# Three small changes of order in one kernel of attention and two expert layers: the held expert's products, the comparisons of the routing, and two places of weights

## The chip, the cores and the metric

The kernel runs on one core of a Trainium2 chip. The metric is the device time of one execution in microseconds (us), as the median of a few runs. The core's engines have queues of their own: TensorE (PE in the profile, with its weight loads as PEld), VectorE (DVE), ScalarE (ACT), GpSimd (POOL) and SyncE (SP), which here issues most transfers.

## What is computed

Three layers follow each other on 1152 tokens of 512 features.

```
x   = attention(q, k, v, s)                  # 2 x 8 heads, 576 positions, causal, a bias from s
e   = argmax(x @ w_gate)                     # first expert layer: one of 8 experts for each token
x1  = gate * (relu(x @ w1[e]) @ w2[e])       # at most 288 tokens for one expert
l   = x1 @ w_gate2                           # second layer: logits over 8 experts
# all (token, expert) pairs in falling order of l: a token takes the expert if it has
# none yet and the expert has fewer than 144 tokens
out = relu(x1 @ w1b[e2]) @ w2b[e2]           # 144 tokens for each of 8 experts
```

Each expert has a w1 of 512 x 1024 and a w2 of 1024 x 512 in f32, 2 MB each, 32 matrices in all.

## The kernel before

**Order.** The schedule is written out by hand: each engine runs its instructions in the order in which the program states them, and waits by semaphores where data or a buffer is missing. So a line that stands earlier in the program is earlier in the queue of its engine, and whatever stands behind a waiting instruction waits with it.

**Stages.** Attention runs until about 140 us. Then `for e in range(E)` runs the first layer's eight experts (146 to 270 us): `layer1` forms relu(x w1) in four steps of two column blocks, `second1` multiplies by w2. Then comes the routing's first phase (270 to 292 us), and from 298 us the second layer, `moe2`, in which the routing's later phases (`phases`, one `yield` at a time) run between the experts' products.

**Weights.** `load_part` fetches a matrix in four parts of 512 KB on SP's queue. `place(i)` says which 2 MB buffer matrix i goes to (i = 2e is w1 of expert e, i = 2e + 1 its w2): `ring[0]` and `ring[1]` exist from the start, `ring[2]`, `ring[3]`, `kept[0]` and `kept[1]` are laid where attention's tiles were, after `at.close()`. `load_next` issues parts in the order of `loads` as long as `free(i)` allows the next one and the expert's number is known; `quota` limits their number. One matrix that may not go stops all behind it. Before, w1 of the third expert (i = 4) goes to `ring[1]`, which holds w2 of the first, and so waits until `second1` of the first expert is over (`0 in given`). The f32 parts are split into a high half (ACT, line 160) and a low half (DVE, line 164) by `split_next`, at places of the experts' steps given in STEPS. The ACT's queue so holds splits, which wait for a transfer, ahead of the `h` and `y` copies that PE waits for.

**The held expert.** The last expert's second product (`held_steps`) is kept back and cut into 24 steps: 4 steps of 6 matmuls for each of 4 column blocks, with an ACT and a DVE step (`y`) behind each pair of blocks (20 steps), then `rows_steps`, 4 steps: 8 transposes on PE, then an ACT copy into `xo` and a scatter of rows to `x2d` in DRAM (`back1_out`, POOL line 1101), for each half of the tokens. FILL says after which step of the routing how many of them ("f") are issued; "r" are the same row steps of the expert before it.

**The routing's first phase.** For each of nine tiles of 128 tokens `compare(t)` writes a 128 x 1152 table of f16 (DVE line 1580; ACT line 1578 for tiles 1, 4 and 7) into one of five buffers `g`, and `products(g, t)` multiplies it on PE (line 1586, nine matmuls). The tiles come in the order 0 1 2 4 3 7 5 6 8. Comparisons were issued four tiles ahead of the products, in each round ahead of the products of that round. The maximum over the counts, the choice of the first full expert (`evi`), its weights (`known(0)`, two parts), and its token numbers (`tok`) follow. `gather` (POOL line 1443) reads the chosen rows from `x2d`, and so waits for all scatters into it. Behind the two gathers POOL writes a word `gone`, for which SP waits in `passed(9)` before it issues the next nine parts of weights. `warm(n)` issues n matmuls of 512 columns with no use but to occupy PE; WARM2 has their numbers at three places, the last ahead of `spread`, which turns the gathered rows for the second layer's first expert.

Of the kernel before, what the change touches and what calls it, by code (L numbers as in the profile page):

```python
# [9 lines left out]
F32 = mybir.dt.float32  # L10
F16 = mybir.dt.float16
BF16 = mybir.dt.bfloat16
# [9 lines left out]
def tile_attention_moe_moe(ctx: ExitStack, tc: tile.TileContext, q, k, v, s, wg1, w1a, w2a, capacity,  # L22
                           wg2, w1b, w2b, out, dbg=None):
    nc = tc.nc
    B, H, S, D = q.shape
    NTOK, DM = out.shape
    E = wg1.shape[1]
# [47 lines left out]
    ring = [ring_pool.tile([P, 4096], F32, name=f"wf{i}") for i in range(2)]  # L75
# [3 lines left out]
    WSP = [tuple(wsp0.tile([P, 4096], t, name=f"{n}{i}") for n, t in (("wh", F16), ("wl", BF16))) for i in range(2)]  # L79
    WS = {}  # L80

    FILL = ". rf rrrf ffff ffffff ffff ffff . . ff ff . . . . ."

# [7 lines left out]

    ONE = (E - 2, E - 1)

    WARM2 = (6, 5, 4)


    order = {}
# [5 lines left out]
    quota = [99]  # L105


    given = set()

    def place(i):  # L110

        e, k = divmod(i, 2)
        if k:
            return (ring[2:] + kept[:1])[(e - 1) % 3] if e else ring[1]
        return ring[(e + 1) % 2 if 0 < e < E else e % 2]

    def load_part(i, c):
        w, k = halves[i]
        t = loaded[i] = place(i)
        e = order[i // 2]  # L120
        src = (w[e:e + 1] if isinstance(e, int) else w[bass.ds(e, 1)]).rearrange("o (c p) f -> p (o c) f", p=P)
        n, f = src.shape[1:]
        t = t.rearrange("p (c f) -> p c f", c=n)
        if i // 2 == E:
            sl = (slice(None), slice(None), slice(c * f // 4, (c + 1) * f // 4))
        else:
            sl = (slice(None), slice(c * n // 4, (c + 1) * n // 4))
        nc.sync.dma_start(t[sl], src[sl])

    def free(i):  # L130

        e, k = divmod(i, 2)
        busy = lambda j: any(x[0] == j for x in split_queue + late)
        if k:
            return e == 0 or len(ring) > 2 and (e < 4 or e - 3 in given)
        return e == 0 or (0 in given if e == 2 else not busy(i - 2 if e == 1 else i - 4))

    def load_next():

        while quota[0] and loads:  # L140
            i = loads[0][0]
            if not (i < 2 or free(i)):
                break
            if i // 2 not in order and not (i < 2 * E and asked and asked[0](i // 2)):
                break
            load_part(*loads.pop(0))
            quota[0] -= 1

    def split_parts(i, part):
        x = loaded[i], *WS[i]  # L150
        if i % 2:
            return [a[:, part * 1024:(part + 1) * 1024] for a in x]
        return [a.rearrange("p (c f) -> p c f", c=4)[:, :, part * 256:(part + 1) * 256] for a in x]

    def split_hi(i, part):
        if part == 0:
            e, k = divmod(i, 2)
            WS[i] = (WSH if e in HELD else W2S[e % 2]) if k else WSP[e % 2]
        src, hi, lo = split_parts(i, part)
# [713 lines left out]
    if "XR" in dbg:  # L873
# [11 lines left out]
    kept = [wsp.tile([P, 4096], F32, name=f"wf{i}") for i in range(4, 6)]  # L885

    W2S = [tuple(kept[1].bitcast(t)[:, 4096 * i + j:4096 * i + j + 2048] for t, j in ((F16, 0), (BF16, 2048)))
           for i in range(2)]
    WSH = ring[1].bitcast(F16)[:, :4096], ring[1].bitcast(BF16)[:, 4096:]

    def open_pools(st, p, tag, names):
        for n, b in names:
# [106 lines left out]
    SL = C0 // 2  # L999
# [43 lines left out]
    mo1, mo2 = {}, {}  # L1043
# [42 lines left out]
    def back1_pe(ys, q_, x2f, l3):  # L1086
        w = x2f.shape[0]
        sl = slice(q_ * w, (q_ + 1) * w)
        for cp in range(2):
            pb = pbs.tile([P, 512], F32)[:w, :2 * (P + 2 * E)].rearrange("p (c d) -> p c d", c=2)  # L1090
            for c in range(2):
                nc.tensor.matmul(pb[:, c], ys[0][:, 2 * cp + c, sl], IW[:, 2 * cp + c], start=True, stop=False)
                nc.tensor.matmul(pb[:, c, :P + E], ys[1][:, 2 * cp + c, sl], IW[:, 2 * cp + c, :P + E],
                                 start=False, stop=True)
            nc.scalar.activation(x2f.rearrange("p (c d) -> p c d", c=4)[:, 2 * cp:2 * cp + 2], pb[:, :, :P],
                                 AF.Copy)
            nc.vector.reduce_sum(l3[:, cp], pb[:, :, P:].rearrange("p c (k e) -> p e c k", k=2), axis=AX.XY)  # L1097

    def back1_out(t, g, xo):
        nc.gpsimd.tensor_scalar(xo[:, DM + E:], g, 1.0 / XSC, None, op0=OP.mult)  # L1100
        i = nc.gpsimd.indirect_dma_start(  # L1101
            out=x2d[:, :], out_offset=bass.IndirectOffsetOnAxis(ap=t, axis=0),
            in_=xo, in_offset=None, bounds_check=NTOK - 1, oob_is_err=False)
        for o in scat2:
            tc.declare_no_dep(i.ins, o.ins, reason="distinct rows")
        scat2.append(i)

    def back1(ys, q_, t, g):


        w = g.shape[0]
        x2f, xo, l3 = (mo1["o"].tile([SL, n], F32, name=a)[:w]
                       for a, n in (("x2f", DM + E + 1), ("xo", DM + E + 1), ("l3", 3 * E)))
        x2f = x2f[:, :DM]
        l3 = l3.rearrange("p (k e) -> p k e", k=3)
        xo16 = xo.bitcast(F16)
        back1_pe(ys, q_, x2f, l3)
        nc.vector.tensor_add(l3[:, 2], l3[:, 0], l3[:, 1])
        nc.vector.tensor_scalar(xo[:, DM:DM + E], l3[:, 2], g, 1.0 / SG, op0=OP.mult, op1=OP.mult)
        nc.vector.tensor_copy(xo16[:, :DM], x2f)  # L1120
        nc.vector.tensor_sub(xo16[:, DM:2 * DM], x2f, xo16[:, :DM])
        back1_out(t, g, xo)

    def slots(r, q_):
        w = CAPS[r] // 2
        return tix[:w, r, q_:q_ + 1], gs[:w, r, q_:q_ + 1]
# [130 lines left out]
            yield from rows_steps(e, ys)  # L1257

    def rows_steps(e, ys):
        for q_ in range(NQ):  # L1260
            t, g = slots(e, q_)
            w = g.shape[0]
            xo = mo1["o"].tile([SL, DM + E + 1], F32, name=("xo", "x2f")[q_])[:w]
            pb = pbs.tile([P, 512], F32).bitcast(F16)[:w]
            for k in range(2):
                for c in range(4):
                    nc.tensor.transpose(pb[:, (4 * k + c) * P:(4 * k + c + 1) * P], ys[k][:, c, q_ * w:(q_ + 1) * w], ident)
            yield
            nc.scalar.activation(xo.bitcast(F16)[:, :2 * DM], pb, AF.Copy)
            nc.gpsimd.memset(xo[:, DM:DM + E], 0.0)  # L1270
            back1_out(t, g, xo)
            yield

    fills = FILL.split()

    def fill():
        for c in fills.pop(0):
            next(todo[c], None)
# [123 lines left out]
    rf = ctx.enter_context(tc.tile_pool(name="routef", bufs=1))  # L1402
# [158 lines left out]
    def ranks(pc, m, Bo, Bh, n, act_t, apart=3):  # L1561


        order = [t for t in range(n) if t not in act_t]
        for k, t in enumerate(act_t):
            order.insert(min(apart * k + apart - 1, len(order)), t)

        def head(first):
            for t in act_t:
                nc.tensor.matmul(pc, ones, Bh[:, t, None, :].to_broadcast([P, n, E]), start=first,  # L1570
                                 stop=False, skip_group_check=True)
                nc.tensor.matmul(pc[:, t], negi, Bh[:, t], start=False, stop=False, skip_group_check=True)
                first = False

        def compare(t):
            g = gp.tile([P, NTT, P], F16, name="g")[:, :n]
            if t in act_t:
                nc.scalar.activation(g, rowb[:, :n], AF.Sign, bias=m[:, t:t + 1], scale=-1.0)
            else:
                nc.vector.tensor_scalar(g, rowb[:, :n], m[:, t:t + 1], None, op0=OP.is_lt)  # L1580
            return g

        def products(g, t):
            rhs = Bh if t in act_t else Bo
            for i in range(n):
                nc.tensor.matmul(pc[:, i], g[:, i], rhs[:, t], start=False,
                                 stop=t == order[-1] and i == n - 1, skip_group_check=True)
        return head, order, compare, products
# [47 lines left out]
    def warm(n):  # L1636

        o = Banks("C1").tile([P, 512], F32)
        for _ in range(n):
            nc.tensor.matmul(o, ident, iotat[:, :512], start=True, stop=True)  # L1640
# [7 lines left out]
    head, tiles, compare, products = ranks(pc, m, Bo, Bh0, NTT, (1, 4, 7), 2)  # L1648
# [1 line left out]
    nc.gpsimd.tensor_sub(sres[:, 0], L2T, S3[:, 0])  # L1650
    nc.gpsimd.tensor_copy(S3[:, 1], sres[:, 0])
    nc.gpsimd.tensor_sub(S3[:, 2], sres[:, 0], S3[:, 1])
    AHEAD = 4
    gs_ = [compare(t) for t in tiles[:AHEAD]]
    head(True)
    for k, t in enumerate(tiles):
        if k + AHEAD < NTT:
            gs_.append(compare(tiles[k + AHEAD]))
        products(gs_[k], t)
        fill()  # L1660
    mx = rw.tile([P, NTT], F32, name="mx0")
    nc.vector.reduce_max(mx, pc, axis=AX.X)
# [23 lines left out]
    fill()  # L1686
    warm(WARM2[0])
    slot_pe(O0, R0, NTT)
    warm(WARM2[1])
    fill()  # L1690
# [241 lines left out]
    pop_lo()  # L1932
    warm(WARM2[2])
    XT1[0] = spread(xg.pop(0))
# [64 lines left out]
```

## Time and profile before

| | |
|---|---|
| time, median of 3 runs | 458.85 us (458.82 to 460.01) |
| the profiled execution: its own time | 456.74 us |
| its span, first to last instruction | 454.7 us |
| PE busy | 400.4 us, 88% of the span |
| PEld, DVE, ACT, POOL busy | 371.6, 309.2, 249.1, 190.9 us |
| DMA | 103.02 MB, mean 227 GB/s |

The span is that of the one execution that was profiled, and all positions below are us from its start. The shares are means over stages with different limits, so a stage is read by its own rows. Line numbers (L164) are those of the kernel before.

### The profile page before, as it was taken

The page shows a single profiled execution, that of the slowest core. Times are in us where ns is not written, and L with a number is a line of the kernel's source. Part 1 is how long each engine was busy: PE and PEld are TensorE (multiplying, and loading weights), DVE is VectorE, ACT ScalarE, POOL GpSimd, SP SyncE. Part 2 cuts the span into 40 slices and gives each one's busy share as a digit, 9 for nine tenths or more (in the row PEclk, how much of TensorE's full clock was granted, in tenths as well). Part 3 has the DMA queues.
Part 4 walks back from the last instruction along what each step waited for, and adds up shares of the span by engine and source line. Part 5 has one row for each costly group of instructions (what it writes and reads, how often), then busy time and mean ns, then how long its engine had stood idle before and what let it go on. Part 6 is the DMA issues. An engine that isn't in the chain of part 4 may idle for free. (4 is left out here: it accounts for less than half of the span.)

```text
span 454.7 us, 13676 instructions
## 1 busy us (share of the span) xinstructions
PE 400.4 (88%) x5260; PEld 371.6 (82%) x5260; DVE 309.2 (68%) x926; ACT 249.1 (55%) x459; POOL 190.9 (42%) x306
## 2 busy tenths in 40 slices
PE   1679999978989998999999999679989999999970
PEld 1457888867767998999999988379889999999960
DVE  7889999987776466876888956775855465465100
ACT  4447888855761546556667727153666466355420
POOL 4387888858822511402412624402432341441120
PEclk9979999989999999999999999969999999999995
DMA  7797999858915599999997930499996978987000
GB/s 156 170 206 175 194 223 223 208 157 274 329 32 224 157 343 400 346 349 353 385 318 167 155 63 27 129 274 319 371 391 176 334 246 262 311 294 246 30 25 20
DMA packets 94398, 103.02 MB, mean 227 GB/s; under 512 B 56136, under 2 KB 63304, under 8 KB 94323
## 3 DMA queue, kind: packets, MB, share of 16 engines
q1 hardware_dynamic: 88931, 91.85, 69.7%
q0 software_dynamic: 4192, 9.91, 7.1%
q8 instruction: 43, 0.70, 0.7%
q10 hardware_dynamic: 1200, 0.30, 0.3%
q14 instruction: 32, 0.26, 0.2%
HBM read 81.42 MB, written 14.59 MB: 211 GB/s over the span
## 5 line engine op out<-in xcount | busy, mean ns | idle before, releaser
L164 DVE TENSOR_TENSOR wl<-wf,wh 128x1024 bf16<-128x1024 f32 x64 | 77.7, 1234 | 25.0 <-ACT wh L160 23.9
L160 ACT ACTIVATE wh<-wf 128x1024 f16<-128x1024 f32 x64 | 65.7, 1051 | 23.5 <-DMA wf<-in_moe_w_dram 23.5
L988 PE MATMUL C<-h,wf 128*128 128x160 f32 (+7 forms) x544 | 58.6, 269 | 1.7 <-ACT h L942 1.7
L933 PE MATMUL A<-xt,wl 128*128 128x144 f16 (+4 forms) x288 | 59.5, 231 | 0.0
L931 PE MATMUL A<-xt,wh 128*128 128x144 f16 (+4 forms) x288 | 59.5, 231 | 0.0
L932 PE MATMUL A<-xt,wh 128*128 128x144 f16 (+4 forms) x288 | 59.5, 231 | 0.0
L1101 POOL DMA_INDIRECT x2d<-xo,tix x14 | 23.0, 1640 | 78.0 <-DVE l L1097 40.2
L932 PEld LDWEIGHTS <-wh 128*128 128x128 f16 x512 | 50.7, 99 | 1.1 <-issue 0.6
L933 PEld LDWEIGHTS <-wl 128*128 128x128 bf16 x512 | 50.8, 99 | 0.9 <-DVE wl L164 0.9
L931 PEld LDWEIGHTS <-wh 128*128 128x128 f16 x512 | 50.8, 99 | 0.2 <-issue 0.2
L536 ACT ACTIVATE pf<-pE,XB 128x512 f32<-128x512 f32 (+4 forms) x80 | 36.9, 515 | 9.7 <-PE pE L531 9.4
L1872 POOL DMA_INDIRECT out_dram<-x2f,tok x14 | 14.9, 1066 | 61.9 <-ACT h L942 34.3
L414 POOL TENSOR_TENSOR pl<-pf,ph 128x512 f16<-128x512 f32 x30 | 35.5, 1194 | 5.8 <-DVE ph L403 3.7
L988 PEld LDWEIGHTS C<-h,wf 128*128 128x128 f32 x256 | 36.2, 190 | 1.9 <-ACT h L942 1.9
L1852 PE MATMUL C<-h,wf 128*128 128x144 f32 x256 | 35.5, 290 | 2.0 <-ACT h L942 2.0
L488 DVE CUSTOM_DVE_ANT_0 junk<-pM,cb 128x128 f16<-128x128 f32 (+4 forms) x80 | 32.2, 431 | 6.5 <-PE pM L478 5.8
L1443 POOL DMA_INDIRECT xg<-x2d,tok x16 | 23.4, 1465 | 26.1 <-PE A L1145 8.9
L1852 PEld LDWEIGHTS C<-h,wf 128*128 128x128 f32 x256 | 32.5, 190 | 2.2 <-ACT h L942 2.2
L476 PE MATMUL pM<-al,ar 128*128 128x128 f16 (+2 forms) x96 | 27.5, 327 | 6.7 <-DVE rm L488 6.5
L559 PE MATMUL pog<-vf,pf 128*128 128x65 f32 x180 | 28.7, 282 | 0.0
L933 PE MATMUL C<-xt,wl 128*128 128x144 f16 x128 | 25.3, 230 | 0.7 <-DVE wl L164 0.7
L932 PE MATMUL C<-xt,wh 128*128 128x144 f16 x128 | 25.3, 230 | 0.0
(410 smaller groups left out, 1167.8 us busy)
## 6 DMA issues: line engine op xcount, KB each, us to landing
wf<-in_moe_w_dram SPq DMA_DIRECT2D x128, 512.0 KB, 10.0
xd<-zero SPq DMA_DIRECT2D x18, 257.0 KB, 4.5
cb<-cumd SPq DMA_DIRECT2D x16, 288.0 KB, 5.5
x2d<-zero SPq DMA_DIRECT2D x9, 260.5 KB, 3.4
kf<-in_k_dram SPq DMA_DIRECT2D x16, 128.0 KB, 4.4
vf<-in_v_dram SPq DMA_DIRECT2D x16, 128.0 KB, 4.3
qf<-in_q_dram SPq DMA_DIRECT2D x14, 128.0 KB, 3.2
bl<-al SPq DMA_DIRECT2D x16, 72.0 KB, 5.2
```

The source lines that it names most:

```text
L160: nc.scalar.activation(hi, src, AF.Copy)
L164: nc.vector.tensor_sub(lo, src, hi)
L414: (nc.gpsimd if ENG[name][i % 2] == "P" else nc.vector).tensor_sub(o, x, y)
L476: nc.tensor.matmul(o, AR[m][:, t * P:(t + 1) * P], AL[m][:, j0:j1], start=True, stop=not diag)
L488: nc.vector.tensor_tensor_reduce(junk[:w, :j1 - j0], o, CB[m][:w, j0:j1], 1.0, r if t == 4 and j0 == 0 else -3e38, OP.add, OP.max, r)
L536: nc.scalar.activation(d, o, AF.Exp, bias=x, scale=2.0 ** -13)
L559: nc.tensor.matmul(o, pf[:, c:c + P], VF[n % 4][:, j, h], start=False, stop=j == t)
L931: nc.tensor.matmul(ph[:, g], wh[:, c, fs], xt[:, c], start=c == 0, stop=False)
L932: nc.tensor.matmul(ph[:, g], wh[:, c, fs], xt[:, 4 + c], start=False, stop=False)
L933: nc.tensor.matmul(ph[:, g], wl[:, c, fs], xt[:, c], start=False, stop=c == 3)
L988: nc.tensor.matmul(py[:, g], a[:, f, d], b[:, f], start=k == 0, stop=k == len(terms) - 1)
L1852: nc.tensor.matmul(py[:, g], a[:, f, d], b[:, f], start=k == 0, stop=k == len(terms) - 1)
```

## The change

`place` exchanges two homes: the w1 matrices that went to `ring[1]` go to `kept[0]`, and the w2 matrices that went to `kept[0]` (fourth and seventh expert, and their like in the second layer) go to `ring[1]`, as does what follows from it in `free`: the third expert's w1 no longer waits for the first expert's w2, the fourth expert's w2 does. The held expert's split w2 (`WSH`) moves to `kept[0]`. Four parts of weights (w2 of the second expert) are issued as soon as the new buffers are declared, ahead of the loads of tokens. FILL puts 14 steps of the held expert, all that is left of its products, behind the products of the first tile, and its four row steps behind the fifth and sixth tile instead of the sixth and seventh. Comparisons go five tiles ahead, each issued behind a round's products. `rows_steps` issues POOL's memset and its scaling of the gates for both halves ahead of the transposes. The last of the three `warm` calls has 5 matmuls instead of 4.

```diff
--- before.py
+++ after.py
@@ -79,7 +79,7 @@
     WSP = [tuple(wsp0.tile([P, 4096], t, name=f"{n}{i}") for n, t in (("wh", F16), ("wl", BF16))) for i in range(2)]
     WS = {}
 
-    FILL = ". rf rrrf ffff ffffff ffff ffff . . ff ff . . . . ."
+    FILL = ". rf rrrf ffff ffffffffffffff . . . ff ff . . . . . ."
 
 
 
@@ -93,7 +93,7 @@
 
     ONE = (E - 2, E - 1)
 
-    WARM2 = (6, 5, 4)
+    WARM2 = (6, 5, 5)
 
 
     order = {}
@@ -111,8 +111,8 @@
 
         e, k = divmod(i, 2)
         if k:
-            return (ring[2:] + kept[:1])[(e - 1) % 3] if e else ring[1]
-        return ring[(e + 1) % 2 if 0 < e < E else e % 2]
+            return (ring[2:] + ring[1:2])[(e - 1) % 3] if e else ring[1]
+        return kept[0] if ((e + 1) % 2 if 0 < e < E else e % 2) else ring[0]
 
     def load_part(i, c):
         w, k = halves[i]
@@ -132,8 +132,8 @@
         e, k = divmod(i, 2)
         busy = lambda j: any(x[0] == j for x in split_queue + late)
         if k:
-            return e == 0 or len(ring) > 2 and (e < 4 or e - 3 in given)
-        return e == 0 or (0 in given if e == 2 else not busy(i - 2 if e == 1 else i - 4))
+            return e == 0 or len(ring) > 2 and (e < 3 or e - 3 in given)
+        return e == 0 or (len(ring) > 2 if e == 2 else not busy(i - 2 if e == 1 else i - 4))
 
     def load_next():
 
@@ -886,7 +886,11 @@
 
     W2S = [tuple(kept[1].bitcast(t)[:, 4096 * i + j:4096 * i + j + 2048] for t, j in ((F16, 0), (BF16, 2048)))
            for i in range(2)]
-    WSH = ring[1].bitcast(F16)[:, :4096], ring[1].bitcast(BF16)[:, 4096:]
+    WSH = kept[0].bitcast(F16)[:, :4096], kept[0].bitcast(BF16)[:, 4096:]
+
+    quota[0] = 4
+    load_next()
+    quota[0] = 99
 
     def open_pools(st, p, tag, names):
         for n, b in names:
@@ -1096,8 +1100,10 @@
                                  AF.Copy)
             nc.vector.reduce_sum(l3[:, cp], pb[:, :, P:].rearrange("p c (k e) -> p e c k", k=2), axis=AX.XY)
 
-    def back1_out(t, g, xo):
+    def back1_gate(g, xo):
         nc.gpsimd.tensor_scalar(xo[:, DM + E:], g, 1.0 / XSC, None, op0=OP.mult)
+
+    def back1_out(t, xo):
         i = nc.gpsimd.indirect_dma_start(
             out=x2d[:, :], out_offset=bass.IndirectOffsetOnAxis(ap=t, axis=0),
             in_=xo, in_offset=None, bounds_check=NTOK - 1, oob_is_err=False)
@@ -1119,7 +1125,8 @@
         nc.vector.tensor_scalar(xo[:, DM:DM + E], l3[:, 2], g, 1.0 / SG, op0=OP.mult, op1=OP.mult)
         nc.vector.tensor_copy(xo16[:, :DM], x2f)
         nc.vector.tensor_sub(xo16[:, DM:2 * DM], x2f, xo16[:, :DM])
-        back1_out(t, g, xo)
+        back1_gate(g, xo)
+        back1_out(t, xo)
 
     def slots(r, q_):
         w = CAPS[r] // 2
@@ -1257,18 +1264,22 @@
             yield from rows_steps(e, ys)
 
     def rows_steps(e, ys):
+        xs = []
         for q_ in range(NQ):
             t, g = slots(e, q_)
-            w = g.shape[0]
-            xo = mo1["o"].tile([SL, DM + E + 1], F32, name=("xo", "x2f")[q_])[:w]
+            xo = mo1["o"].tile([SL, DM + E + 1], F32, name=("xo", "x2f")[q_])[:g.shape[0]]
+            nc.gpsimd.memset(xo[:, DM:DM + E], 0.0)
+            back1_gate(g, xo)
+            xs.append((t, xo))
+        for q_, (t, xo) in enumerate(xs):
+            w = xo.shape[0]
             pb = pbs.tile([P, 512], F32).bitcast(F16)[:w]
             for k in range(2):
                 for c in range(4):
                     nc.tensor.transpose(pb[:, (4 * k + c) * P:(4 * k + c + 1) * P], ys[k][:, c, q_ * w:(q_ + 1) * w], ident)
             yield
             nc.scalar.activation(xo.bitcast(F16)[:, :2 * DM], pb, AF.Copy)
-            nc.gpsimd.memset(xo[:, DM:DM + E], 0.0)
-            back1_out(t, g, xo)
+            back1_out(t, xo)
             yield
 
     fills = FILL.split()
@@ -1650,13 +1661,13 @@
     nc.gpsimd.tensor_sub(sres[:, 0], L2T, S3[:, 0])
     nc.gpsimd.tensor_copy(S3[:, 1], sres[:, 0])
     nc.gpsimd.tensor_sub(S3[:, 2], sres[:, 0], S3[:, 1])
-    AHEAD = 4
+    AHEAD = 5
     gs_ = [compare(t) for t in tiles[:AHEAD]]
     head(True)
     for k, t in enumerate(tiles):
+        products(gs_[k], t)
         if k + AHEAD < NTT:
             gs_.append(compare(tiles[k + AHEAD]))
-        products(gs_[k], t)
         fill()
     mx = rw.tile([P, NTT], F32, name="mx0")
     nc.vector.reduce_max(mx, pc, axis=AX.X)
```

## Rows read from the trace of the kernel before

**Rows 1.** Windows of three stretches: busy us (instructions) by engine, PEclk, DMA share, GB/s

```profile
300.00:333.00 33.00, 29.58 (x410) 28.44 (x409) 23.80 (x99) 16.19 (x29) 8.78 (x12) 0.94 1.05 337
333.00:440.00 107.00, 105.78 (x1317) 104.51 (x1315) 52.59 (x170) 55.02 (x92) 32.06 (x33) 1.00 0.71 234
```

**Rows 2.** Waits of PE, 160 to 200 us: us in total, times, longest

```profile
PE C L988 <- ACT h L942: 1.7, 1, 1.7
PE D L1093 <- DVE y L991: 0.6, 1, 0.6
```

**Rows 3.** Timeline of ACT, 145 to 190 us: start, us, operation [idle before]

```profile
161.51 1.06 ACT L160 ACTIVATE wf<-wf 128x1024 f16<-128x1024 f32 x1 [1.65 <-DMA wf<-in_moe_w_dram]
...
171.80 1.06 ACT L160 ACTIVATE wh<-wf 128x1024 f16<-128x1024 f32 x1 [2.86 <-DMA wf<-in_moe_w_dram]
```

**Rows 4.** Timeline of SP's DMA queue, 100 to 260 us

```profile
134.67 1.97 SPq L128 DMA_DIRECT2D wf<-in_moe_w_dram  x4
151.96 1.37 SPq L1014 DMA_TRANSPOSE xt<-xd  x1
...
154.83 2.89 SPq L128 DMA_DIRECT2D wf<-in_moe_w_dram  x4
...
162.56 16.12 SPq L128 DMA_DIRECT2D wf<-in_moe_w_dram  x16
```

**Rows 5.** Timeline of PE, 160.5 to 174.5 us, up to the second expert

```profile
160.32 1.39 PE L988 MATMUL C<-h,wf 128*128 128x160 f32 x9
```

**Rows 6.** Line L1014 (transposed loads of tokens), issue to landing

```profile
DMA to landing us min/median/max: 7.1/9.2/11.1
```

**Rows 7.** Timeline of PE, 275 to 300 us

```profile
277.01 1.58 PE L1249 MATMUL C<-h,wf 128*128 128x136 f16 x24
278.43 0.37 PE L1586 MATMUL A<-Bh,g 128*128 128x8 f16 x9
...
280.31 0.87 PE L1249 MATMUL C<-h,wf 128*128 128x136 f16 x12
...
281.69 0.75 PE L1267 MATMUL D<-ident,y 128*68 128x128 f16 x8
```

**Rows 8.** Timeline of DVE, 240 to 302 us

```profile
275.90 2.28 DVE L1580 TENSOR_SCALAR g<-rowb,m 128x1152 f16<-128x1152 f32 x3 [1.38 <-ACT rowb L1148]
...
281.64 0.44 DVE L1255 SCALAR_TENSOR_TENSOR y<-C,y 128x272 f16<-128x272 f32 x1 [1.86 <-ACT y L1253]
282.00 1.54 DVE L1580 TENSOR_SCALAR g<-rowb,m 128x1152 f16<-128x1152 f32 x2
```

**Rows 9.** Timeline of POOL, 240 to 302 us

```profile
284.45 1.18 POOL L1101 DMA_INDIRECT x2d<-xo,tix  x1 [4.57 <-ACT x2f L1269]
...
286.28 1.55 POOL L1101 DMA_INDIRECT x2d<-x2f,tix  x1 [0.31 <-POOL x2f L1100]
292.81 1.06 POOL L1443 DMA_INDIRECT xg<-x2d,tok  x1 [4.98 <-DVE Bo L1739]
```

**Rows 10.** DMA issues, 284 to 294 us: median us to landing

```profile
x2d<-x2f,tix POOLq DMA_INDIRECT x1, 5.7
```

**Rows 11.** Half-microsecond windows around the fall of PE's clock

```profile
297.00:297.50 0.50, 0.07 (x2) 0.07 (x3) 0.09 (x1) 0.00 (x0) 0.00 (x0) 0.91 0.23 33
...
304.00:304.50 0.50, 0.50 (x9) 0.50 (x7) 0.50 (x5) 0.00 (x0) 0.00 (x0) 0.76 1.16 290
```

**Rows 12.** Timeline of PE, 275 to 300 us, behind the routing's first phase

```profile
293.06 1.03 PE L1640 MATMUL C<-iotat,ident 128*128 128x512 f16 x4
296.20 0.56 PE L1463 MATMUL A<-ident,xg 72*128 72x72 f16 x8 [2.12 <-ACT rowb L1148]
```

**Rows 13.** Timeline of SP's DMA queue, 296 to 300 us

```profile
296.15 5.66 SPq L128 DMA_DIRECT2D wf<-in_moe_w_dram  x5
```

**Rows 14.** Timeline of ACT, 300 to 345 us

```profile
331.13 1.06 ACT L160 ACTIVATE wh<-wf 128x1024 f16<-128x1024 f32 x1 [4.17 <-DMA wf<-in_moe_w_dram]
```

**Rows 15.** Timeline of PE, 332 to 338 us

```profile
332.54 0.76 PE L1852 MATMUL C<-h,wf 128*128 128x144 f32 x4 [1.97 <-ACT h L942]
```

## The prediction

> **What bounds the kernel now.** I read the page first: PE is busy for 88% of the span, and a kernel like that is bounded by PE wherever PE has no gap. So the next view is the list of PE's own gaps, stage by stage. Between 146 and 284 us they are few. In the first experts two stand out, 1.7 us and 0.6 us [rows 2]. The reader should see that both are named after an engine (ACT's `h`, DVE's `y`), though neither engine is short of time. ACT's timeline says what it did instead: at 171.80 a split of weights had waited 2.86 us for its transfer, at 161.51 another 1.65 us [rows 3], and the `h` and `y` copies stood behind them in ACT's queue. The queue of SP gives the origin: after the second expert's w1 at 134.67 nothing is issued until the loads of tokens at 151.96; w2 of the second expert goes at 154.83 and the third expert's w1 as late as 162.56 [rows 4].
>
> The second place is the routing's first phase. PE is nearly full until its last products, and then a chain of waits sets when the second layer begins. POOL's timeline shows its tail: the scatter of the held expert's second half starts at 286.28, and the first gather at 292.81 [rows 9]. The name behind that wait (a DVE operation) had long been done; the scatter takes 5.7 us to land [rows 10], which is 291.98, and from there to the gather's start are 0.8 us. Behind the two gathers SP is released and resumes the weights at 296.15 [rows 13].
>
> The third place is the beginning of the second layer. From 300 to 333 us the DMA share is 1.05 at 337 GB/s [rows 1]; at 331.13 ACT had waited 4.17 us for weights [rows 14], and PE 1.97 us for ACT [rows 15]. From 333 to 440 us PE is busy for 105.78 of 107 us [rows 1]. So what counts for the end is not when PE enters the second layer but when the weights of its third expert arrive, and these come from a stream that resumes at 296.15.
>
> **The change, part by part.**
>
> *Places of weights.* No operation is added or removed: the same 2 MB transfers go to other buffers. The third expert's w1 no longer waits for the first expert's w2 to be used, and the four parts of the second expert's w2 are issued where SP's queue was empty, from about 137 us (134.67 + 1.97, rows 4) instead of 154.83. The third expert's w1 then follows the loads of tokens at about 155 instead of 162.56. Seven us are more than both of ACT's waits (2.86 and 1.65 us, rows 3), so I take both PE gaps as gone: −1.7 − 0.6 = −2.3 us [rows 2]. What is late next? `ring[1]` now makes the fourth expert's w2 wait for the first expert, but that matrix stood behind the same wait before, as everything did. Loads of tokens now stand behind eight more parts on SP (for the third expert), which is not used until the second expert is over. The bounds are 0 (the parts do not come earlier) and −2.3 us; I take the latter, because the gaps have no second cause in the rows.
>
> *The held products.* Work is moved, not removed. Before, 60 matmuls ran in three batches from 277.01 with the products of two tiles between them; 24 take 1.42 us (277.01 to 278.43), a tile 0.23 us (278.43 to the next batch), and the last 12, which start at 280.31, end at 281.02 [rows 7]. In one piece they end at 277.01 + 60/24 × 1.42 = 280.56, 0.46 us earlier. DVE's `y` came 0.62 us behind their end (281.64) [rows 8], so now at 281.18.
>
> *The comparisons.* Being five ahead costs nothing by itself: `g` has five buffers, and the buffer is released by the same products as before. But DVE's queue now reads three comparisons, the two `y`, three comparisons. Before it was three, `y`, one, `y`, two. Behind the last `y` there are now three at 2.28 us instead of two at 1.54 us [rows 8]. The last comparison ends at 281.18 + 0.36 + 2.28 = 283.82 instead of 282.00 + 1.54 = 283.54: +0.3 us for the routing's maximum and for all that waits for it (counts, first full expert, its first two parts of weights). What hides these 0.3 us: the gather does not wait for the counts but for the scatter, and the stream behind it resumes by the gather. Without that cover they would be paid in full.
>
> *The rows and the scatter.* The transposes of the held rows began at 281.69 behind six tiles' products [rows 7]; now they stand behind five, at 280.56 + 4 × 0.23 = 281.48, with `y` complete some 0.4 us earlier. I take 0.3 us, so the first scatter starts at 284.15 instead of 284.45. The second starts today 0.65 us after the first ends (284.45 + 1.18 = 285.63 to 286.28, rows 9), because memset and scaling lie between; with both issued ahead only the wait of 0.31 us in its row is left, and it starts at 284.15 + 1.18 + 0.31 = 285.64, 0.64 us earlier. Landing after the same 5.7 us, it releases the gathers and then the stream 0.6 us earlier. Bounds: 0, if the landing is set by something else, and 1 us, if the scatter also lands faster away from the first weights. I take −0.6.
>
> One page would have it otherwise: the Trainium skill, "DMA: Bandwidth & Descriptors", section "Anatomy of one DMA — SWDGE (gpsimd) path", gives such a transfer about 2.0 us plus its bytes at 436 GB/s. For 68 rows of some 2 KB that is an estimate of 2.3 us, by which the scatter would have landed at 288.6, the gather would be waiting for something else, and the sum would lose its 0.6 us. The 5.7 us of rows 10 decide.
>
> *One more warm matmul.* Four of them took 1.03 us from 293.06; a fifth adds 0.26 us in a pause of PE that lasted until 296.20 [rows 12]. It costs nothing there. It might matter for the clock: that was at 2.4 GHz until 297.4 (0.91 granted in that half microsecond) and at 1.2 GHz until 304.2 (0.76 in that one) [rows 11], 6.8 us in which half the speed, 3.4 us of work, was lost. But PE reached its wait at 332.54 before its weights all the same, so by rows 14 and 15 an earlier PE would mostly wait longer. I take 0 of 3.4.
>
> **Sum.** −1.7 − 0.6 (first experts) − 0.6 (stream of the second layer) = −2.9 us. The profiled execution would go from 456.74 to 453.8 us. The median of the runs lies 2.1 us above it, which none of these rows explains; I take the difference off the median: 458.85 − 2.9 = 455.9 us.
>
> **Rivals.** A change of less than 0.3% (1.4 us) cannot be told from none here.
>
> *The clock stays up.* If PE's pause ahead of the second layer shrinks enough, the clock does not fall, the routing's next two phases, which name the second layer's next experts, come up to 3.4 us sooner, and with them part of the stream. For it: rows 11 and 12. Against it: the DMA queues are full from 300 to 333 us [rows 1]. About half of the 3.4 us would be kept: −2.9 − 1.6 = −4.5, 454.4 us. The Trainium skill, "TensorE: Matmul & The Clock Gate", Part 1, has activity release the throttle, which speaks for it; this trace agrees as far as the fall came behind a pause of PE.
>
> *Only one place pays.* The scatter's landing is not what holds the gather, or the first experts' 2.3 us are half lost to a new wait of ACT: −2.3 + 0.3 or about −2.0, 456.8 us.
>
> *The change does not do what it says.* If the new buffers lie on attention's tiles that are read until 152 us, the early parts are not early. Then only the 0.6 us and perhaps the small gap remain, less 0.3: 458.4 us.
>
> *Slower: tokens behind weights.* SP's queue is in order. If the four early parts still stand there at 151.96, the load of the second expert's tokens goes 2.89 us later [rows 4], behind 2.1 MB, which at 337 GB/s [rows 1] take 6.2 us, and lands 7.1 to 11.1 us after its issue [rows 6]. PE wants it at 160.32 + 1.39 = 161.7 [rows 5]. From 151.96 and 7.1 there are 2.6 us to spare; at worst PE stands 6.4 us. It decides from a stall of 4.3 us (2.9 gained, 1.4 more); taken with 4.5 to 5, the time is 460.5 us. Against it: the first of those buffers lies where attention's first tiles of queries, keys and values are, whose last use in the program is some heads before its end.
>
> **How the numbers follow.** Chances: forecast 0.50, clock stays up 0.14, one place only 0.12, not what it says 0.16, slower 0.08. The first three make it faster by over 0.3% (0.76), the fourth stays within (0.16), the last is slower (0.08). The predicted time is the likeliest case's, 455.9 us. The range reaches from below the rival with the clock (454.4, less 0.8 us for a scatter that lands faster and for the spread of the runs) to the case of no effect: 453.6 to 458.6 us.
>
> **What will show it.** ACT's splits at about 158 to 172 without a wait for weights, and PE's two gaps gone: the first step is right. SP's issue of four parts before 145 us: the places do what they say. DVE's three comparisons in one piece behind the second `y`, ending about 0.3 us later relative to the first held product, with the second scatter 0.6 us earlier: the routing is read rightly. A gather that starts less than 1 us behind the scatter's landing: the chain is right. And ACT still waiting for weights ahead of the third expert of the second layer, whatever the clock did: the clock is worth little. The prediction is wrong if PE shows a new gap ahead of the second expert, if the gather does not move, or if the wait for weights at 331 us moves by another amount than the gather.

## The result, and the profile after

| | median of the runs | profiled execution | its span |
|---|---|---|---|
| before | 458.84 us (458.46 to 460.01) | 456.74 us | 454.7 us |
| after | 453.12 us (451.90 to 454.15) | 452.32 us | 450.4 us |

The ratio is 0.9862, with a 95% interval of 0.9826 to 0.9898: 6.3 us faster (4.7 to 8.0), where 2.9 were forecast. The profiled executions differ by 4.4 us only. Ratios, here and below, leave out runs that lie over 1.5% above the fastest of the same kernel, and medians do not. The forecast of 455.9 us had the right side and too small a gain, and the time lies just below its range.

What the change says it does, it does, though the early parts go later than forecast. SP's queue after, to be held against [rows 4]; the second row, from a narrower window, shows the last four of the eight parts alone, and the row in the block below it is the wait of SP's queue ahead of them (us in total, times, longest):

```profile
134.79 11.10 SPq L128 DMA_DIRECT2D wf<-in_moe_w_dram  x8
143.79 2.11 SPq L128 DMA_DIRECT2D wf<-in_moe_w_dram  x4
156.76 1.29 SPq L1018 DMA_TRANSPOSE xt<-xd  x1
...
160.04 4.28 SPq L128 DMA_DIRECT2D wf<-in_moe_w_dram  x8
```

```profile
SPq L128 <- DVE ka L646: 6.5, 1, 6.5
```

Eight parts, not four, stand ahead of the loads of tokens. The first four are the second expert's w1, at 134.79 us as before. The second expert's w2 follows from 143.79 us, 11 us ahead of its place before (154.83): SP first waited 6.5 us for an operation of attention on DVE (`ka`, line 646). The third expert's w1 is issued from 160.04 instead of 162.56. ACT's timeline after shows what came of it at the two splits of [rows 3]:

```profile
158.70 1.99 ACT L160 ACTIVATE wf<-wf 128x1024 f16<-128x1024 f32 x2
...
168.94 1.05 ACT L160 ACTIVATE wh<-wf 128x1024 f16<-128x1024 f32 x1
```

There is no bracket behind the operations, so ACT did not wait ahead of them. The view of PE's waits, which showed the two gaps of [rows 2], is empty for 160 to 200 us. The loads of tokens go out later (156.76 instead of 151.96), and no gap of PE follows from that.

In the routing, PE's timeline after answers to [rows 7], with the held products in one piece:

```profile
275.54 3.71 PE L1256 MATMUL C<-h,wf 128*128 128x136 f16 x60
...
279.99 0.61 PE L1279 MATMUL D<-ident,y 128*68 128x128 f16 x8
```

DVE's timeline after answers to [rows 8]: three comparisons stand behind the last `y`, and the maximum behind them:

```profile
279.71 0.44 DVE L1262 SCALAR_TENSOR_TENSOR y<-C,y 128x272 f16<-128x272 f32 x1 [1.17 <-ACT y L1260]
280.07 2.27 DVE L1591 TENSOR_SCALAR g<-rowb,m 128x1152 f16<-128x1152 f32 x3
282.82 0.23 DVE L1673 TENSOR_REDUCE mx<-A 128x9 f32<-128x72 f32 x1 [0.47 <-PE A L1597]
```

POOL's timeline after answers to [rows 9], the DMA issues after to [rows 10]:

```profile
282.62 1.18 POOL L1107 DMA_INDIRECT x2d<-xo,tix  x1 [4.86 <-ACT x2f L1281]
284.09 1.10 POOL L1107 DMA_INDIRECT x2d<-x2f,tix  x1 [0.30 <-issue]
289.78 1.66 POOL L1454 DMA_INDIRECT xg<-x2d,tok  x1 [4.58 <-DVE g L1719]
```

```profile
x2d<-x2f,tix POOLq DMA_INDIRECT x1, 4.8
```

Times here are best read against the routing's first transposes of its matrices (274.06 us before, 272.40 after), since what lies ahead moved too. From there the maximum comes after 10.42 us (9.95 before, 284.01), the second scatter after 11.69 (12.22 before), the gather after 17.38 (18.75 before). The first scatter comes 0.17 us earlier (10.22 against 10.39). The second scatter landed in 4.8 us instead of 5.7.

At the start of the second layer, windows after that answer to [rows 11], and the third expert's split and PE's two longest gaps, which answer to [rows 14, 15]:

```profile
296.50:297.00 0.50, 0.50 (x20) 0.50 (x18) 0.50 (x2) 0.50 (x2) 0.00 (x0) 0.88 1.08 373
...
300.00:300.50 0.50, 0.50 (x8) 0.50 (x7) 0.50 (x5) 0.50 (x1) 0.00 (x0) 0.71 1.15 318
```

```profile
326.33 1.06 ACT L160 ACTIVATE wh<-wf 128x1024 f16<-128x1024 f32 x1 [1.39 <-DMA wf<-in_moe_w_dram]
```

```profile
303.11 0.24 PE L937 MATMUL C<-xt,wl 128*128 128x144 f16 x1 [1.49 <-DVE wl L164]
...
317.67 1.04 PE L1152 MATMUL A<-identf,m 128*128 128x128 f32 x5 [1.17 <-ACT xt L1477]
```

Ahead of the second layer the clock stood at 1.2 GHz for 3.4 us instead of 6.8. But in the changed kernel's trace it had also fallen for 3.4 us in the routing, where the kernel before had kept 2.4 GHz. The same window, before and then after:

```profile
283.00:287.00 4.00, 2.65 (x45) 1.63 (x42) 3.42 (x17) 1.46 (x2) 2.24 (x4) 1.00 0.08 15
```

```profile
283.00:287.00 4.00, 3.63 (x34) 1.92 (x34) 2.65 (x18) 0.00 (x0) 1.89 (x2) 0.57 0.23 55
```

PE no longer waits at the third expert, but its waits before it grew: 1.49 us and 1.17 us, where the kernel before had 0.67 and 0.41 at the same places.

### The profile page after: what moved, and what is told of

The parts are those of the page before. It is cut to its first block, busy times and chain, and to the rows that moved or that the text cites. A ratio compares the mean times of both kernels' runs of the same rounds, so it can differ in the third digit from the quotient of the medians.

```text
span 450.4 us, 13683 instructions
## 1 busy us (share of the span) xinstructions
PE 401.7 (89%) x5261; PEld 372.3 (83%) x5261; DVE 309.1 (69%) x926; ACT 248.8 (55%) x459; POOL 192.4 (43%) x306
## 5 line engine op out<-in xcount | busy, mean ns | idle before, releaser
L1883 POOL DMA_INDIRECT out_dram<-x2f,tok x14 | 16.4, 1170 | 63.4 <-ACT h L946 28.4
```

## The experiments

Three theories were held against each other at first. The first: the steps of the forecast, each worth what it says. The second: the clock ahead of the second layer brings what the forecast missed. The third: the exchange in the second layer does. Four chips were met; A is the chip of the first four experiments, B, C and D those of the later ones. The chip of the two kernels above is not on record; their traces look like those of A (below). A single trace stands behind each reading of a stretch; the ratios rest on 6 to 12 runs of each variant.

| kernel | chip | median, us | before there, us | ratio (95%) |
|---|---|---|---|---|
| e1, places and early parts | A | 453.04 | 458.83 | 0.9906 (0.9873 to 0.9939) |
| e2, routing alone | A | 456.41 | 458.83 | 0.9943 (0.9916 to 0.9970) |
| e3, fifth warm matmul alone | A | 458.28 | 458.83 | 0.9998 (0.9973 to 1.0023) |
| e4, 14 warm matmuls | A | 459.20 | 458.83 | 1.0028 (1.0000 to 1.0055) |
| e5, rows and scatters ahead alone | B | 460.26 | 461.10 | 0.9964 (0.9919 to 1.0008) |
| e6, order of products and comparisons alone | B | 460.74 | 461.10 | 0.9968 (0.9929 to 1.0006) |
| e7, exchange in the first layer alone | B | 460.72 | 461.10 | 0.9982 (0.9949 to 1.0015) |
| e8, before with PE's gap filled | B | 463.06 | 461.10 | 1.0037 (1.0005 to 1.0070) |
| e9, whole change | C | 460.24 | 461.06 | 0.9988 (0.9966 to 1.0011) |
| e10, as e1 | C | 460.65 | 461.06 | 0.9984 (0.9956 to 1.0013) |
| e11, as e7 | C | 460.95 | 461.06 | 1.0003 (0.9981 to 1.0026) |
| e12, whole, four first parts | C | 462.38 | 461.06 | 1.0031 (1.0007 to 1.0056) |
| e15, whole change | D | 460.39 | 460.93 | 1.0036 (0.9991 to 1.0082) |

### One part of the change at a time (e1 to e4)

e1 is the kernel before with the edits to `place`, `free` and `WSH`, and the early load. e2 has the edits to `rows_steps`, `back1_out`, `FILL` and `AHEAD` alone. e3 and e4 change one number each:

```
-    WARM2 = (6, 5, 4)
+    WARM2 = (6, 5, 5)      # e3
+    WARM2 = (6, 5, 14)     # e4
```

> The places of weights alone (with the four parts issued early), routing and warm matmuls as before. First theory (the predicted steps were right, the weights of the second layer follow the gather one to one): PE's two gaps in the first experts go, 2.3 us less than before, and the wait for weights in the third expert of the second layer stays at about 2 us of PE. Second theory (the clock ahead of the second layer is what gave the unforeseen part): also 2.3 us, since neither the pause nor the warm matmuls are touched. Third theory (the second layer's weights land faster because their buffers were exchanged too): 4 us or more, with PE's gap in the third expert gone.

> The routing alone: held products behind the first tile, comparisons five ahead, memset and gates ahead of the transposes; places and warm matmuls as before. First theory: 0.6 us less than before, all of it through an earlier gather. Second theory: 1 to 2.5 us less, in runs where the clock falls for a shorter time ahead of the second layer. Third theory: 0.6 us less.

> One more warm matmul alone, everything else as before. First theory: no difference within 0.3 us. Second theory: up to 1.5 us less, if 0.26 us of occupied PE are enough to keep the clock. Third theory: no difference.

> Fourteen warm matmuls instead of four at the last place, about 2.1 us more of occupied PE in a pause that lasts 2.1 us, everything else as before: the clock should not fall ahead of the second layer. First theory: no gain (within 0.5 us), PE only waits longer for the weights of the third expert. Second theory: 1.5 to 3 us less than before, with the phases, the second gather and the weights behind it earlier by as much. Third theory: no difference.

By their ratios the places bring 4.3 us (0.94% of 458.83, interval 2.8 to 5.8) and the routing 2.6 us (0.57%, interval 1.4 to 3.9); both are larger than forecast (2.3 and 0.6), and together, 6.9 us, they account for the whole within these intervals. The fifth warm matmul brings nothing that can be measured.

The second theory falls with e4. Two windows of it show that the clock stayed at 2.4 GHz where the kernel before had lost 3.4 us of work (it fell once earlier, from 287 to 291 us, as in the routing of the changed kernel):

```profile
296.00:300.00 4.00, 3.82 (x27) 2.03 (x25) 1.39 (x2) 2.77 (x4) 1.92 (x5) 1.00 0.34 93
300.00:304.00 4.00, 2.95 (x62) 2.69 (x63) 3.41 (x8) 2.85 (x4) 0.00 (x0) 1.00 0.99 315
```

Its time did not fall, and PE's timeline in e4 says where 2.0 us of the clock's gain went, into longer waits for the split of weights and for tokens (0.67 and 0.41 us before):

```profile
308.48 0.24 PE L933 MATMUL C<-xt,wl 128*128 128x144 f16 x1 [2.07 <-DVE wl L164]
...
322.90 1.04 PE L1145 MATMUL A<-identf,m 128*128 128x128 f32 x5 [1.03 <-ACT xt L1466]
```

That the places brought more than forecast is in part explained by the kernels with the old places, e2 to e4. PE's waits from 145 to 200 us, first in e2, then in e3, then in e4:

```profile
PE C L988 <- ACT h L942: 3.0, 1, 3.0
```

```profile
PE C L988 <- ACT h L942: 2.4, 1, 2.4
PE D L1093 <- DVE y L991: 0.4, 1, 0.4
```

```profile
PE C L988 <- ACT h L942: 2.7, 1, 2.7
```

The wait that was 1.7 us in the profile of before [rows 2] is 2.4 to 3.0 us in three other executions of the same code of this stretch. Both waits together, which the forecast took at 2.3 us, come to 2.7 to 3.0 us there. And the long one drags something along: windows of e3 around it.

```profile
172.00:174.00 2.00, 0.66 (x2) 0.67 (x3) 1.01 (x1) 2.00 (x3) 0.36 (x1) 0.73 1.06 405
174.00:176.00 2.00, 2.00 (x14) 1.89 (x14) 1.95 (x3) 1.17 (x2) 0.29 (x1) 0.50 1.07 403
176.00:178.00 2.00, 2.00 (x20) 1.96 (x19) 0.62 (x1) 0.41 (x2) 0.00 (x0) 0.91 1.04 411
```

The clock fell to 1.2 GHz behind the wait, in e3 and in e4, for 3.4 us, which is 1.7 us of work lost; in the profiled execution of before it had not. From attention's last products (line L652) to the routing's first transposes of its matrices the kernel before took 132.05 us, e2 132.47, e3 133.77, e4 134.12; with the new places e1 took 128.99 and the whole change 129.48. So in this stretch the places are worth 2.6 us against the profiled execution and up to 5.1 us against others.

That is not all of e1's gain. From the routing's first transposes to its end the kernel before took 180.66 us, e3 179.34 and e4 178.69, but e1 178.08, although its gather starts no earlier than theirs (18.76 us behind the transposes). The wait of PE at the second layer's third expert (1.97 us before [rows 15], 1.5 us in e2, none in e3 and e4) is gone in e1. How e1's 4.3 us divide between the two layers was not measured on chip A: no run there has the first layer's exchange alone.

### Halves of the parts, and the gap filled (e5 to e8)

e5 takes memset and scaling ahead of the scatters, as the change does, and leaves order and comparisons; e6 changes `FILL`, `AHEAD` and the order of products and comparisons alone. e7 has the early parts and the new places of the first layer, but the second layer's as before. e8 is the kernel before with seven matmuls without use (512 columns) at the place of PE's gap. The core of e7:

```
-            return (ring[2:] + kept[:1])[(e - 1) % 3] if e else ring[1]
-        return ring[(e + 1) % 2 if 0 < e < E else e % 2]
+            return (ring[2:] + (ring[1:2] if e < E else kept[:1]))[(e - 1) % 3] if e else ring[1]
+        if e >= E:
+            return ring[e % 2]
+        return kept[0] if ((e + 1) % 2 if 0 < e < E else e % 2) else ring[0]
```

> The rows' steps alone: memset and gates of both halves ahead of the transposes, so that the second scatter follows the first at once; fills, comparisons, places and warm matmuls as before. Theory of the scatter (its landing holds the gather, and it lands faster when the two scatters follow each other closely, by some 0.9 us): the second scatter starts 0.35 us earlier, the gather 1.2 us earlier relative to the routing's start, and the time falls by 1 us or a little more. Rival (the landing is faster because the first weights come later behind longer comparisons): the gather moves by 0.35 us only, and so does the time.

> The fills and the comparisons five ahead alone, the rows' steps as before. Theory of the scatter: the first scatter starts some 0.2 us earlier, the second too, landing as before (5.7 us), the time falls by 0.2 us or not at all, with the routing's maximum 0.4 us later. Rival: the gather starts about 1 us earlier and the time falls by 1 us, since the first weights, which go 0.4 us later, no longer meet the scatter.

> The exchange of places with the four early parts in the first layer alone; the second layer's matrices go where they went before. Theory of the varying gap (what the first experts lose is 1.7 to 3.0 us of waiting from one execution to the next, and 1.7 us more where the clock falls in it, so that 4 us are gained on average): as much faster as the whole exchange was, about 4.3 us. Rival (the exchange in the second layer brings the third expert's weights earlier): about 2.3 us, the rest missing.

> The kernel before with seven matmuls of no use (512 columns, about 1.5 us together) on PE at the start of the second expert's second product, ahead of the place where PE waits for the split of the third expert's weights. No transfer is moved. Theory of the varying gap: PE's wait there shrinks by 1.5 us, the clock does not fall there, and the time falls by what the clock cost on average, 0.5 to 1 us. Rival (the wait alone is the cost, the clock never mattered there): no change within 0.3 us, or 0.2 us slower.

On chip B no part gave a measurable gain, the first layer's exchange included; e7's interval leaves out the 4.3 us of e1. The intervals of e5 and e6 are wide enough to hold what e2 gained on A, so whether the routing gains there was not settled by them. e5 and e6 both shorten the way from the second scatter to the gather (6.53 us before; 5.99 in e5, 5.94 in e6, 5.64 in e2 with both), so the two halves share that gain. In e5 the gather gains 0.9 us against the first scatter, where 1.2 against the routing's start were expected; in e6 it starts 0.96 us earlier, as the rival had it, though not for the rival's reason: the first weights follow the second scatter after 1.47 us there, as in the kernel before. e8 was meant to fill a gap, and there was none to fill: its matmuls came on top. Chip B differed from A in a way that later runs made plain.

### The whole beside its parts on one chip (e9 to e12)

e9 is the changed kernel, e10 is e1, e11 is e7. e12 is the changed kernel with

```
-    quota[0] = 2
+    quota[0] = 4
     known(0)
...
-    passed(9)
+    passed(7)
```

> The whole change once more, beside its parts on one chip. First theory (the gain is mostly PE's stall in the first experts, which varies from run to run and from chip to chip, plus the earlier gather): 0.986 to 0.992 of before on a chip where the first experts stall, 0.992 to 0.996 on one where they don't; first expert's start to the routing's first matrices 123 to 125 us, third expert of the second layer without a stall of over 0.5 us. Rival (the second layer's places bring the part that the forecast missed): the ratio is the same on either chip, and e11 falls short of it by 2 us or more.

> The exchange of places in both layers with the early parts, routing as before. First theory: behind the whole change by what the earlier gather is worth, 1.4 to 2.6 us, and equal to e11 within 0.3%. Rival (second layer's places): ahead of e11 by 1.4 us or more.

> The exchange in the first layer alone, the second layer's places as before. First theory: equal to e10 within 0.3%, since kernels with the old places also reached the third expert of the second layer without a stall. Rival: slower than e10 by 1.4 us or more, with PE waiting over 1 us at that expert.

> The whole change, but four parts instead of two of the first full expert's weights are issued when that expert is known, and seven instead of nine behind the gathers: 1 MB more in the stretch in which the scatter lands. If the first parts delay the scatter (the reason given for 4.8 instead of 5.7 us of landing), it lands in over 5.5 us and the gather starts 0.7 us or more later against the routing's start; the time is within 0.3% of e9 or above it. If the landing is the scatter's own, it stays at 4.8 us, the first split of the second layer comes sooner, and the time is up to 1.5 us below e9.

e10 and e11 agree within 0.3%, as the first theory has it, so the third theory falls as far as it asked for a lead of 1.4 us or more; e3 and e4, with the old places, also reached the second layer's third expert without a wait of PE. A smaller share of the second layer's places is not excluded: four of the twelve traces with the old ones there show a wait of PE at that expert (0.65 us in e11 to 1.97 us before), and of the six with the new ones only e12. But on chip C the whole change has no measurable gain either: 0.9988, where 0.992 to 0.996 had been expected of a chip without the stall, and e10 is not the expected 1.4 to 2.6 us behind it.

e12 settled another question and gave a surprise. If the first weights held up the scatter, twice as many should have held it up more; the gather, which waits for it, started 17.34 us behind the routing's first transposes, as in e9 (17.43). It was the gathered rows themselves that came late. DMA issues of e9, then of e12, and PE's wait in e12:

```profile
xg<-x2d,tok POOLq DMA_INDIRECT x2, 3.3
```

```profile
xg<-x2d,tok POOLq DMA_INDIRECT x2, 7.1
```

```profile
305.43 0.66 PE L1474 MATMUL A<-ident,xg 72*128 72x72 f16 x8 [4.13 <-DMA xg<-x2d,tok]
```

### The kernel before on such a chip (e13 to e16)

e13, e14 and e16 are the kernel before, unchanged; e15 is the whole change, all on chip D. (Of e15 the medians lie 0.5 us the other way than its ratio, which the interval covers.)

> The kernel before, unchanged, to see its stalls in more executions than one. If the first experts' stall is the kernel's own and only its size varies: PE's waits for ACT's h and DVE's y between the first expert's start and 180 us sum to 1.7 to 3 us where PE starts the first expert without an issue wait, and under 0.5 us where it lost 2 us to one (the weights are then there). If the gain is given back later instead, these waits are there on either chip, and the whole change shows new waits behind 270 us.

> The same kernel again: first expert's start to the routing's rows within 1 us of e13 if the stall is set by the chip, 1 to 4 us apart if it varies from execution to execution.

> The whole change on the same chip. If that chip has the issue wait at the first expert: ratio 0.995 to 1.0; if it has none: 0.984 to 0.991, with 123 to 124 us from the first expert's start to the routing's rows against 126 to 129 in e13 and e14. If the gain is given back later, the ratio is the same on either chip.

> A third execution of the kernel before, for the spread: as e14.

The three profiled executions took 462.17, 463.19 and 460.47 us. All PE waits of e14 from 145 to 200 us:

```profile
PE A L931 <- issue: 1.0, 1, 1.0
PE pE L652 <- DVE ka L646: 0.6, 1, 0.6
PE A L933 <- issue: 0.5, 1, 0.5
PE A L932 <- issue: 0.4, 1, 0.4
```

The two waits of [rows 2] are not there, as had been expected of a chip on which PE loses 2 us to "issue". Instead PE lost 1.9 us within the first expert's first products, to a wait for nothing that the profile shows. ACT's splits of the second expert's w2 and of the third expert's w1, late in [rows 3], had their data when ACT came to them:

```profile
167.49 1.99 ACT L160 ACTIVATE wf<-wf 128x1024 f16<-128x1024 f32 x2
...
177.73 1.05 ACT L160 ACTIVATE wh<-wf 128x1024 f16<-128x1024 f32 x1
```

The whole change has the same wait there (in e9):

```profile
PE A L935 <- issue: 2.2, 3, 1.1
```

A second wait marks these chips, inside attention: PE waits once for ACT for 3.1 to 4.6 us in all twelve traces of B, C and D, and in none of the six of A and of the result. In e16:

```profile
PE pM L476 <- ACT pf L536: 4.1, 1, 4.1
```

It lies ahead of the stretch compared here, and the change does not touch it. So on B, C and D PE is already about 2 us late within this stretch when the weights would have stopped it, and the earlier weights buy nothing measurable. In e16, which lost the least to "issue" (1.7 us), ACT still waited 0.46 us for the third expert's w1, and PE did not. In e14 the clock then fell, as the granted clock in this window shows:

```profile
158.00:160.00 2.00, 2.00 (x18) 2.00 (x16) 0.52 (x1) 1.38 (x2) 1.04 (x8) 0.50 0.40 73
```

It did so in four of the six traces with the old places (e5, e6, e13, e14; not e16, nor e8 with its added matmuls, whose clock fell at 272 us), and in none of the six with the new ones. From L652 to the routing's first transposes those four took 133.15 to 133.57 us, e16 131.52, and the six 131.58 to 131.89. Without the fall of the clock the two versions of this stretch are equal on these chips, as far as the one trace e16 can tell. Whether the places have a part in that fall was not tested.

## Why the prediction had the right side and the wrong size

**Places of weights: mechanism right, size wrong.** The early parts went out from 143.79 us, not from about 137, since SP waited 6.5 us for DVE's `ka`: the ground of the rival "the change does not do what it says" was there, but it only took 7 us off a lead that was still long enough. The third expert's w1 went from 160.04, not at about 155. ACT's waits and both gaps are gone, and tokens behind weights, the rival with a loss, did not occur. The term that failed is "−1.7 − 0.6 = −2.3 us", with the reason "the gaps have no second cause in the rows". The sizes came from a single execution, which was a favourable one. The warning stood in the text: the median lay 2.1 us above the profile, "which none of these rows explains", and I took the difference off the median all the same. On chip A part of that difference can be this very gap: up to 3.0 us where 2.3 were taken, and in two of four traces a fall of the clock of 1.7 us on top. The places measured 4.3 us there by e1's ratio; the traces give 2.6 to 5.1 us in the term's own stretch, and by the traces some of the gain lies in the second layer, for which the term had nothing.

**Landing of the scatter: the lower size taken.** The second scatter came 0.53 us earlier against the routing's start (0.64 forecast), but it also landed in 4.8 us instead of 5.7, and the gather started 1.37 us earlier instead of 0.6, which is beyond even the bound of 1 us that I had named. The routing alone measured 2.6 us by e2's ratio; of these the gather's start shows 1.4, and where the rest comes from was not shown (the interval reaches down to 1.4). The reason given with it, distance from the first weights, is not borne out by e6 (the same distance as before, and yet a shorter way to the gather) nor by e12; why the landing is shorter stays open. The Trainium skill, "DMA: Bandwidth & Descriptors", section "Anatomy of one DMA — SWDGE (gpsimd) path", by which 2.3 us were estimated for such a transfer, is not borne out by any run: 4.4 to 5.7 us were measured.

**Routing's maximum: right.** It came 0.47 us later (0.3 forecast), and the gather hides it.

**Clock ahead of the second layer: right.** Worth nothing was forecast, and e4 kept the clock up and gained nothing.

**Third expert: half right.** ACT still waits for weights, 1.39 us instead of 4.17, but PE does not. I had it that the wait moves with the gather, and named the contrary as a sign of being wrong. It came: the wait moved by 4.80 us and the gather by 3.03. With the old places ACT's wait there was 3.65 us in e2, 2.23 in e3 and 1.43 in e4, so one execution does not size this either.

**What stays open.** On B, C and D the earlier gather is there in every trace (17.43 us in e9 and 17.36 in e15 behind the routing's first transposes, 18.76 and 18.74 in e14 and e16), but no ratio of the whole change is off 1 there. In the traces this 1.3 us is not lost again: from the routing's first transposes to the end e9 took 178.94 us and e15 177.98, against 179.22 in e13, 180.22 in e14 and 180.15 in e16. C's interval would hold such a gain (0.28%), D's does not. Whether it is lost in most executions or hidden by their spread stays open. Nor is it shown why PE waits in attention and at the first expert on three chips and not on the fourth. None of the variants tried is measurably faster than the changed kernel; the places alone (e1, e10) come level with it, within the noise.

## What to carry to other kernels

A stall that is the difference of two streams, here PE against arriving weights, has no fixed size: look at it in several executions and on more than one chip before its length goes into a sum, and ask whether the clock falls in it. If the median of the runs lies off the profiled execution by more than the gain in question, look there first. The end of a merged row is worth a look too: eight transfers in one row of 11 us were two groups of 2 us with a wait between them. Here 1 MB of weights moved ahead of a small gather was paid for by the gather's landing.

## What the runs showed of the hardware that I had not expected

The same program met the first expert without a loss on one chip and with 1.7 to 2.3 us of PE waiting for "issue" on three others, in every trace, before or after the change, with a wait of 3.1 to 4.6 us in attention besides; the kernel before took 458.8 us on the one and 460.9 to 461.1 on the others. One more megabyte of weights issued ahead of a gather took the gather's landing from 3.3 us (e9) to 7.1 (e12), in one trace each. And a clock held at 2.4 GHz ahead of the second layer (e4) was worth nothing that could be measured (ratio 1.0028, 1.0000 to 1.0055) where PE then waited for weights.
